# The first queries in two pieces, single-chunk transposes for pair 0, and re-placed row copies in a fused attention and gMLP kernel

## The chip, the cores and the metric

The kernel runs on one core of a Trainium2 chip. A core has TensorE (PE in the profile; PEld is its weight load), VectorE (DVE), ScalarE (ACT), GpSimd (POOL) and SyncE (SP, which here only issues transfers), and 16 DMA engines. The metric is the device time of one execution in microseconds (us); less is better.

## The reference

Block-sparse attention over 4 batches of 8 heads, 768 positions, head size 64, then a gated MLP over the merged heads. The mask works on blocks of 32 positions: 24 by 24 blocks.

```python
scores = scale * np.matmul(q, k.transpose(0, 1, 3, 2))
mask = np.abs(blk_i - blk_j) <= window          # window = 1
mask = mask | (blk_i == 0) | (blk_j == 0) | (blk_i == n_blocks - 1) | (blk_j == n_blocks - 1)
for qb in range(n_blocks):
    for kb in sampled_blocks[qb]:                # 3 sampled blocks for each
        mask[qb * block:(qb + 1) * block, kb * block:(kb + 1) * block] = True
scores = np.where(mask, scores, -1000000000.0)
attn = softmax(scores)
x = (attn @ v), heads merged                     # 4 x 768 x 512
h = np.maximum(x @ w_in, 0.0)                    # u, v = its halves of 512
v_n = (v - mu) / np.sqrt(var + 1e-06)
v_s = np.einsum('ts,bsd->btd', w_spatial, v_n) + b_spatial[None, :, None]
out = (u * v_s) @ w_out
```

## The kernel before

**Layout.** Keys and queries of one head lie in a tile `kq` [128 partitions, 8 heads, 2 x 768 columns]: 64 partitions hold the transposed head vectors (keys in the first 768 columns, queries in the rest), and the other 64 (`MX`) hold mask rows, so that one product of 128 partitions gives score plus mask. The mask rows on the key side are the same for all heads (`K_` columns, a one-hot of the block), and those on the query side are made by products of `bm` with the one-hot rows (`mask_rows`, L268, one for each third of 256 query columns), written into head 0 and copied to the other heads by `rows` (L236). While `mask_rows` uses head 1's columns as its operand, head 1's vector partitions are zero (memset, L173).

**Chunks and pairs.** A head's 768 positions are 6 chunks of 128. Heads are worked in pairs; pair 0 is heads 0 and 1 of batch 0. A load brings float32 rows to `st_k`, `st_q`, `st_v`; a cast makes bfloat16 in `nat`; PE transposes by a product with the identity into PSUM; a DVE copy brings that to `kq`. For pair 0 one transpose takes two chunks of 64 columns at once (`head`, L274), so that even and odd chunks come out in two halves of the partitions and need two copies (`split0`, L280). The load and cast order chunks so that the first four become two runs. Later pairs transpose both heads of a chunk together (`tr_first`, `tr_rest`).

**Order.** The order on each engine is that of the text; a wait stands on the instruction that needs it. The work is cut in slots (the loop at L846). In slots 0 to 35 batch 0 is done in units of three slots: a slot begins with a score product (`qk_unit`, L387), whose four 256-column products of PE are followed by one exp on ACT (L420, 1024 columns; in slot 0 two of 512, L410). Two PSUM buffers hold the scores, so the product of slot s waits for the exp of slot s - 2. Value products (`av_unit`, L444; 24 products of 65 columns in three groups `e` of 8, L458) of the unit follow some slots later; `av_at` (L840) says where: for unit 0 groups 0, 1 and 2 in slots 5, 6 and 6. The functions put in by `when` follow behind them in the slot: `second` (L331: the last two key chunks of head 0) in slot 0, `third` (L337: head 1's keys and first four query chunks) in slot 1, the third mask product in slot 2, `tr_first` of pairs 1, 2, 3 in slots 4, 7 and 9, `tr_rest` of pair 0 in slot 18 (L356, last query third of heads 0 and 1), and the `rows` of later heads (`ROWS`, L733). Units 0 and 1 are heads 0 and 1 with two query thirds; units 2, 3 and 4 are pairs 1 to 3, from slots 6, 9 and 12. From slot 36 on whole heads are worked (L428, L431, L476), and the MLP is dealt in between.

**Queues.** ACT issues the first key load and the first query load (L140, L141); SP issues all else in the order of the text, from L142 on. POOL makes iotas, memsets and the casts, in order (`ORDER`, L304). `filler` products of zeros keep PE busy: 26 ahead, and two at each of three places (`FILL2`). `mhalf` (L172) is the exponent of the MLP's normalization on POOL. The last column of each of six `vv` tiles (values) is set to one (L171), so that the value product also sums the weights.

Of the kernel before, what the change touches and what calls it, by code (L numbers as in the profile page):

```python
# [17 lines left out]
def _listify(ap: bass.AP) -> bass.AP:  # L18
    t = ap.tensor
    if isinstance(t.shape, tuple):  # L20
        t = dataclasses.replace(t, shape=list(t.shape))
        ap = dataclasses.replace(ap, tensor=t)
    return ap
# [3 lines left out]
def kernel(  # L27
# [38 lines left out]
    MOE0 = 12  # L66
    FILL, FILL2 = 26, (2, 2, 2)
    U_DVE = (0, 1, 2, 3, 4, 5)
# [49 lines left out]
    def cast(p, nm, eng, hs=BOTH, cs=ALLC):  # L118
        if nm == "v":
            dst = vv[p % NVV][:, hs, cs, 0:D]  # L120
        else:
            if p not in nat:
                nat[p] = work.tile([128, 2 * NCH, 2, D], BF16, tag="nat", bufs=4, name="nat")
            c0 = 0 if nm == "k" else NCH
            dst = nat[p][:, c0 + cs.start:c0 + cs.stop].rearrange("p c h d -> p h c d")[:, hs]
        src = st[nm, p].rearrange("p h (c d) -> p h c d", d=D)[:, hs, cs]
        if p == 0 and nm != "v":
            dst = nat0_view()[:, hs, (c0 + cs.start) * D:(c0 + cs.stop) * D]
            if cs is not C45:
                dst = dst[:, 0].rearrange("p (i t d) -> p t i d", t=2, d=D)  # L130
                src = src[:, 0].rearrange("p (t i) d -> p t i d", t=2)
            else:
                dst = dst.rearrange("p h (c d) -> p h c d", d=D)
        if eng is nc.scalar:
            nc.scalar.activation(out=dst, in_=src, func=AF.Copy)
        else:
            eng.tensor_copy(out=dst, in_=src)  # L137

    samp = const.tile([KR, 2 * NR], I32)
    load(0, "k", H0, C03, eng=nc.scalar)  # L140
    load(0, "q", H0, C03, eng=nc.scalar)  # L141
    nc.sync.dma_start(out=samp[MR], in_=_listify(sampled_blocks).bitcast(I32))  # L142
    load(0, "k", H0, C45)
    load(0, "k", H1)
# [24 lines left out]
    make_identity(nc, ident)  # L169
    for s in range(NVV):  # L170
        nc.gpsimd.memset(vv[s][:, :, :, D:VA], 1.0)  # L171
    nc.gpsimd.memset(mhalf, -0.5)  # L172
    nc.gpsimd.memset(kq[0:D, 1, 0:TW], 0.0)  # L173

# [69 lines left out]
    act_copy(kq[MX, 0, K_], kq[MX, 1, K_])  # L244
    cast(0, "q", PL, H0, C03)
    cast(0, "k", PL, H0, C45)
# [33 lines left out]
    def split0(ps, h, c0, n, t, copy=dve_copy):  # L280
        w = n * 64
        copy(kq[0:D, h, c0 * 128 + t * w:c0 * 128 + (t + 1) * w], ps[t * D:(t + 1) * D, 0:w])

    K4, K2, Q4 = (0, 2 * TC), (2 * TC, NCH - 2 * TC), (NCH, 2 * TC)
    ps0 = bank()
    head(ps0, 0, *K4)
    split0(ps0, 0, *K4, 0)
    rows(slice(3, 4), K_)
    filler(FILL2[0], wps)
    mask_rows(psum.tile([128, 1024], FP32, tag="sc", bufs=2, name="mq"), 0, act_copy, 1)  # L290
    rows(slice(2, 3), slice(0, 512), nc.scalar)
    filler(FILL2[1], wps)
    psq = bank("psq", "av")
    head(psq, 0, *Q4)
    split0(psq, 0, *Q4, 0)
    split0(ps0, 0, *K4, 1)
    filler(FILL2[2], wps)
    mask_rows(psum.tile([128, 512], FP32, tag=moe_tag(), bufs=1, name="mq"), 1, act_copy, rs=MR)
    split0(psq, 0, *Q4, 1)
    rows(slice(4, 6), K_)  # L300
    rows(H1, qcols(0, 2), PL)
    rows(slice(2, 3), slice(512, S), PL)

# [27 lines left out]
    def second():  # L331
        ps2 = bank("ps2", "av")
        head(ps2, 0, *K2)
        for t in range(2):
            split0(ps2, 0, *K2, t)

    def third():  # L337
        ps1 = bank("ps1")
        head(ps1, 1, 0, NCH)
        head(ps1, 1, *Q4, NCH * 64)  # L340
        for c0, n, at in ((0, NCH, 0), (*Q4, NCH * 64)):
            for t in range(2):
                split0(ps1[:, at:at + n * 64], 1, c0, n, t)

# [8 lines left out]
    def tr_rest(p, t0=1):  # L353
# [3 lines left out]
        if p == 0:  # L357
            for h in range(2):
                head(ps, h, 2 * NCH - 2, 2, h * 128)
            for odd in range(2):  # L360
                dve_copy(kq[0:D, 0:2, S + (NCH - 2 + odd) * 128:S + (NCH - 1 + odd) * 128],
                         ps[odd * D:(odd + 1) * D, 0:256].rearrange("d (h n) -> d h n", h=2))
            return
# [365 lines left out]
    def c(f, *a, **kw):  # L729
        return lambda: f(*a, **kw)  # L730

    K_Q0 = slice(0, S + TW)
    ROWS = [(3, 2, 8, qcols(0)), (5, 6, 8, K_),  # L733
            (15, 4, 6, qcols(1, 2))]
    when(0, second)
    when(4, lambda: rows(slice(6, 8), qcols(1, 2), PL), lambda: casts(-3, None))
# [104 lines left out]
    for u in range(len(UNITS)):  # L841
        for e in range(3):
            sl = (5, 6, 6)[e] if u == 0 else 3 * u + e + (4 if u < 3 else 3)
            av_at.setdefault(sl, []).append((u, e))
    NS = S0 + 12 * (NP - NG)
    for s in range(NS + LAG + 2):  # L846
# [6 lines left out]
        for f in pre.get(s, []):  # L853
            f()
        for u, e in av_at.get(s, []):
            av_unit(u, e)
        if 0 <= s - LAG - S0 and s - LAG < NS:
# [5 lines left out]
        for f in late.get(s, []):  # L863
            f()
        while post:
            post.pop(0)()
# [31 lines left out]
```

## Time and profile before

| | us |
|---|---|
| three runs, median (lowest, highest) | 209.96 (209.9, 210.68) |
| the profiled execution | 210.04 |
| its span, first to last instruction | 208.3 |
| PE busy | 201.0 |
| ACT busy | 168.4 |
| DVE busy | 146.8 |
| POOL busy | 89.4 |

The span is what the profile can show; 1.7 us of the execution lie around it. The granted clock reads 1.00. A busy share is a mean over the whole kernel; at the start, in the first 11 us, no engine is busy throughout, and the parts wait for each other in turn. A row of the timeline shows start, duration, engine, line, operation, output and inputs, shapes, and how many instructions were merged into it; in brackets stands an idle time of the engine ahead of it and what ended it. The rows of the first 11 us, PE's and ACT's in the first 20 us, and DMA's landings are what the change is to be read against.

### The profile page before, as it was taken

Reading aid. Unit: us, or ns where it says so; the run is one execution under the profiler, and the core shown is the slowest. Engines: PE = TensorE matmul, PEld = TensorE weight load, DVE = VectorE, ACT = ScalarE, POOL = GpSimd, SP = SyncE. Lnnn points to the kernel's source line nnn. Section 1 sums busy time; section 2 is a strip of 40 time slices with the busy share of each in tenths; the row PEclk is TensorE's granted clock in tenths of the full one; section 3 lists DMA queues with packets and bytes.
Section 4 is the critical chain, followed back from the end, with each engine's and each line's share of the span. In section 5 each row is a group of like instructions: output and inputs, shape, how many; then the busy total and the mean of one; then the engine's idle time right before and its main releaser. Section 6 shows DMA issues by size and latency. Waiting matters only on the chain.

```text
span 208.3 us, 5489 instructions
## 1 busy us (share of the span) xinstructions
PE 201.0 (97%) x2203; PEld 138.0 (66%) x2225; DVE 146.8 (70%) x315; ACT 168.4 (81%) x222; POOL 89.4 (43%) x186
## 2 busy tenths in 40 slices
PE   6899999999999999999999999999999999999993
PEld 6599888777766776667556676667665567445551
DVE  6888776989876766575975585456875666576871
ACT  6899999999999999989899878889899884266021
POOL 6888989767927964006757600006210000013000
PEclk9999999999999999999999999999999999999999
DMA  5999899999999999499987920499402010610016
GB/s 143 338 362 357 275 383 270 206 247 389 253 253 308 259 300 208 139 199 386 292 176 206 139 41 0 164 189 335 75 0 41 0 37 4 250 57 0 0 70 232
DMA packets 53053, 39.48 MB, mean 190 GB/s; under 512 B 33956, under 2 KB 47652, under 8 KB 53028
## 3 DMA queue, kind: packets, MB, share of 16 engines
q1 hardware_dynamic: 52596, 38.74, 70.0%
q10 hardware_dynamic: 432, 0.39, 0.6%
q8 instruction: 17, 0.28, 0.5%
q14 instruction: 8, 0.07, 0.1%
HBM read 24.77 MB, written 6.29 MB: 149 GB/s over the span
## 4 chain that ended last, share of the span: by engine, by line
PE 87%; DVE 4%; ACT 4%; DMA 2%; issue 1%; POOL 0%; ACTq 0%
PE ps L428 21%; PE ps_moe L630 17%; PE ps_moe L561 13%; PE ps_av L476 12%; PE ps L415 7%; PE ps_av L458 4%; PE ps_t L561 4%; PE ps_t L630 4%; PE ps_sc L630 2%; ACT a_all L420 2%; DVE stats L594 2%; DVE vn L185 2%; DMA st_q<-in_q_dram 2%; PE ps_sc L561 1%; PE ps L263 1%
## 5 line engine op out<-in xcount | busy, mean ns | idle before, releaser
L431 ACT ACTIVATE a_all<-ps 128x768 bf16<-128x768 f32 x144 | 113.4, 812 | 13.8 <-PE ps L428 6.2
L428 PE MATMUL ps<-kq 128*128 128x512 bf16 (+1 forms) x288 | 70.3, 326 | 0.3
L476 PEld LDWEIGHTS <-a_all 128*128 128x128 bf16 x864 | 46.6, 98 | 19.0
L476 PE MATMUL ps_av<-vv,a_all 128*128 128x65 bf16 x864 | 51.1, 194 | 0.1
L428 PEld LDWEIGHTS <-kq 128*128 128x128 bf16 x288 | 27.9, 97 | 23.6
L137 POOL CAST nat<-st_k 128x256 bf16<-128x256 f32 (+3 forms) x37 | 17.7, 509 | 38.7 <-DMA st_k<-in_k_dram 38.7
L420 ACT ACTIVATE a_all<-ps 128x1024 bf16<-128x1024 f32 x35 | 33.5, 1027 | 0.3
L630 PE MATMUL ps_moe<-w_spt,vn 128*128 128x512 bf16 (+1 forms) x144 | 33.1, 325 | 0.0
L598 POOL TENSOR_SCALAR std<-mv 128x3 f32<-128x3 f32 (+1 forms) x9 | 3.4, 376 | 48.7 <-DVE mv L595 48.5
L661 DVE TENSOR_TENSOR sb<-ps_moe,b_row 128x512 f32<-128x512 f32 x18 | 12.4, 690 | 14.5 <-PE ps_moe L630 14.2
L630 PE MATMUL ps_moe<-xt,w_in_t 128*128 128x256 bf16 (+1 forms) x108 | 21.7, 299 | 0.2
L415 PE MATMUL ps<-kq 128*128 128x256 bf16 x135 | 20.8, 275 | 0.8 <-DVE kq L211 0.6
L561 PE MATMUL ps_moe<-w_in_t,xt 128*128 128x512 bf16 x65 | 20.2, 378 | 0.2
L137 POOL CAST vv<-st_v 128x256 bf16<-128x256 f32 (+2 forms) x37 | 18.5, 533 | 3.9 <-DMA st_v<-in_v_dram 3.8
L137 POOL CAST nat<-st_q 128x256 bf16<-128x256 f32 (+2 forms) x41 | 19.2, 496 | 1.6 <-DMA st_q<-in_q_dram 1.5
L561 PE MATMUL ps_moe<-w_out_t,un 128*128 128x512 bf16 x64 | 19.4, 378 | 0.2
L441 DVE TENSOR_TENSOR xn<-ps_av,rc 128x384 bf16<-128x384 f32 (+1 forms) x36 | 18.5, 513 | 1.4 <-DVE rc L440 0.2
L664 DVE TENSOR_TENSOR un<-sb,un 128x512 bf16<-128x512 f32 x24 | 17.4, 727 | 1.5
L630 PEld LDWEIGHTS <-vn 128*128 128x128 bf16 x192 | 15.5, 97 | 4.4
L594 DVE BATCH_NORM_STATS2 stats<-vn 128x6 f32<-128x512 bf16 x24 | 16.5, 688 | 1.5 <-ACT vn L589 0.9
L211 DVE COPY osb<-ps_moe 128x512 f32<-128x512 f32 x12 | 8.3, 689 | 11.2 <-PE ps_moe L561 9.3
L211 DVE COPY kq<-tt 64x1536 bf16<-64x1536 bf16 x24 | 15.4, 641 | 0.6 <-DMA tt<-nat 0.2
(94 smaller groups left out, 241.6 us busy)
## 6 DMA issues: line engine op xcount, KB each, us to landing
out_dram<-osb SPq DMA_DIRECT2D x23, 256.0 KB, 2.1
st_k<-in_k_dram SPq DMA_DIRECT2D x15, 384.0 KB, 4.6
st_v<-in_v_dram SPq DMA_DIRECT2D x15, 384.0 KB, 6.2
st_q<-in_q_dram SPq DMA_DIRECT2D x12, 384.0 KB, 4.9
ws_f<-in_moe_w_spatial_dram SPq DMA_DIRECT2D x6, 384.0 KB, 5.5
w_f<-in_moe_w_in_dram SPq DMA_DIRECT2D x8, 256.0 KB, 6.3
w_f<-in_moe_w_out_dram SPq DMA_DIRECT2D x4, 256.0 KB, 5.4
st_q<-in_q_dram SPq DMA_DIRECT2D x3, 256.0 KB, 6.9
```

What stands on the lines that cost most here:

```text
L137: eng.tensor_copy(out=dst, in_=src)
L211: nc.vector.tensor_copy(out=o, in_=i)
L415: nc.tensor.matmul(out=ps[:, at:at + n * TW], lhsT=kq[:, h, ci * 128:(ci + 1) * 128], rhs=kq[:, h, qcols(t0, n)], start=True, stop=True)
L420: nc.scalar.activation(out=out, in_=ps, func=AF.Exp, scale=0.125)
L428: nc.tensor.matmul(out=ps[:, n0:n1], lhsT=kq[:, j % H, ci * 128:(ci + 1) * 128], rhs=kq[:, j % H, S + n0:S + n1], start=True, stop=True)
L431: nc.scalar.activation(out=a_ref["h", j][:, ci, :], in_=ps[:, 0:S], func=AF.Exp, scale=0.125)
L441: nc.vector.tensor_tensor(out=out, in0=ps[:, :, 0:D], in1=rc[:, 0:n].to_broadcast([128, n, D]), op=ALU.mult)
L476: nc.tensor.matmul(out=av_ref[j][:, qc, :], lhsT=a_ref["h", j][:, ci, qc * 128:(qc + 1) * 128], rhs=vv[p % NVV][:, h, ci, :], start=(ci == ...
L561: nc.tensor.matmul(out=ref["ps"][:, 0:w], lhsT=lhs(i), rhs=rhs(i), start=(i == 0), stop=(i == n - 1))
L594: nc.vector.bn_stats(out=stats, in_=self.vn[:, tcc, :])
L630: nc.tensor.matmul(out=o.rearrange("p (c t) -> p c t", c=n), lhsT=lhs(i)[:, (d0 + x) * 128:(d0 + x + 1) * 128], rhs=rhs(i), start=(i == 0) ...
L664: nc.vector.tensor_tensor(out=self.in_place(*area), in0=sb, in1=self.in_place(*area), op=ALU.mult)
```

## The change

Head 0's first four query chunks come in two loads of two chunks, the first on ACT's queue, the second on SP's, ahead of the keys that SP loads; each has a cast of its own. The two-run order of chunks is kept for head 0's first four key chunks only. The first two mask products, both with head 1's one-hot rows, stand near each other, and the zeroed columns are doubled for that. On ACT both mask copies follow each other without a row copy between them. One filler place goes. Key rows of heads 2 to 7 are copied head by head at more places, all on DVE. Pair 0's later transposes (`second`, `third`, `tr_rest`) take one chunk each (`ones`), so that one copy (`take`) replaces two. The first value group of unit 0 stands at the end of slot 4. Memsets of `vv` 1 to 5 stand with the v casts, and that of `mhalf` in slot 20.

```diff
-    FILL, FILL2 = 26, (2, 2, 2)
+    FILL, FILL2 = 26, (2, 2)
...
         if nm == "v":
             dst = vv[p % NVV][:, hs, cs, 0:D]
+            if 0 < p < NVV:
+                nc.gpsimd.memset(vv[p][:, hs, cs, D:VA], 1.0)
...
-            if cs is not C45:
+            if hs is H0 and cs is C03:
...
     load(0, "k", H0, C03, eng=nc.scalar)
-    load(0, "q", H0, C03, eng=nc.scalar)
+    load(0, "q", H0, C01, eng=nc.scalar)
     nc.sync.dma_start(out=samp[MR], in_=_listify(sampled_blocks).bitcast(I32))
+    load(0, "q", H0, C23)
     load(0, "k", H0, C45)
...
-    for s in range(NVV):
-        nc.gpsimd.memset(vv[s][:, :, :, D:VA], 1.0)
-    nc.gpsimd.memset(mhalf, -0.5)
-    nc.gpsimd.memset(kq[0:D, 1, 0:TW], 0.0)
+    nc.gpsimd.memset(kq[0:D, 1, 0:2 * TW], 0.0)
+    nc.gpsimd.memset(vv[0][:, :, :, D:VA], 1.0)
...
-    cast(0, "q", PL, H0, C03)
+    cast(0, "q", PL, H0, C01)
+    cast(0, "q", PL, H0, C23)
...
+    def ones(ps, h, c0, n, at=0):
+        for i in range(n):
+            tr(ps[0:D, at:at + n * 128], i, nat0_view()[:, h, (c0 + i) * D:(c0 + i + 1) * D])
+
+    def take(ps, h, c0, n):
+        dve_copy(kq[0:D, h, c0 * 128:(c0 + n) * 128], ps[0:D, 0:n * 128])
...
     ps0 = bank()
+    rows(slice(3, 4), K_)
     head(ps0, 0, *K4)
     split0(ps0, 0, *K4, 0)
-    rows(slice(3, 4), K_)
     filler(FILL2[0], wps)
     mask_rows(psum.tile([128, 1024], FP32, tag="sc", bufs=2, name="mq"), 0, act_copy, 1)
-    rows(slice(2, 3), slice(0, 512), nc.scalar)
+    psq = bank("psq", "av")
+    head(psq, 0, NCH, TC)
+    for t in range(2):
+        split0(psq, 0, NCH, TC, t)
+    mask_rows(psum.tile([128, 512], FP32, tag=moe_tag(), bufs=1, name="mq"), 1, act_copy, 1)
+    split0(ps0, 0, *K4, 1)
     filler(FILL2[1], wps)
-    psq = bank("psq", "av")
-    head(psq, 0, *Q4)
-    split0(psq, 0, *Q4, 0)
-    split0(ps0, 0, *K4, 1)
-    filler(FILL2[2], wps)
-    mask_rows(psum.tile([128, 512], FP32, tag=moe_tag(), bufs=1, name="mq"), 1, act_copy, rs=MR)
-    split0(psq, 0, *Q4, 1)
-    rows(slice(4, 6), K_)
+    psr = bank("psr", "av")
+    head(psr, 0, NCH + TC, TC)
+    for t in range(2):
+        split0(psr, 0, NCH + TC, TC, t)
+    rows(slice(2, 3), K_)
     rows(H1, qcols(0, 2), PL)
-    rows(slice(2, 3), slice(512, S), PL)
...
     def second():
         ps2 = bank("ps2", "av")
-        head(ps2, 0, *K2)
-        for t in range(2):
-            split0(ps2, 0, *K2, t)
+        ones(ps2, 0, *K2)
+        take(ps2, 0, *K2)
     def third():
         ps1 = bank("ps1")
-        head(ps1, 1, 0, NCH)
-        head(ps1, 1, *Q4, NCH * 64)
-        for c0, n, at in ((0, NCH, 0), (*Q4, NCH * 64)):
-            for t in range(2):
-                split0(ps1[:, at:at + n * 64], 1, c0, n, t)
+        ones(ps1, 1, 0, NCH + TC)
+        take(ps1, 1, 0, NCH + TC)
+        psr = bank("psr", "av")
+        ones(psr, 1, NCH + TC, TC)
+        take(psr, 1, NCH + TC, TC)
...
             for h in range(2):
-                head(ps, h, 2 * NCH - 2, 2, h * 128)
-            for odd in range(2):
-                dve_copy(kq[0:D, 0:2, S + (NCH - 2 + odd) * 128:S + (NCH - 1 + odd) * 128],
-                         ps[odd * D:(odd + 1) * D, 0:256].rearrange("d (h n) -> d h n", h=2))
+                ones(ps, h, 2 * NCH - TC, TC, h * TW)
+            dve_copy(kq[0:D, 0:2, qcols(2)], ps[0:D, 0:2 * TW].rearrange("d (h n) -> d h n", h=2))
...
-    ROWS = [(3, 2, 8, qcols(0)), (5, 6, 8, K_),
+    ROWS = [(3, 2, 8, qcols(0)), (3, 5, 6, K_), (7, 6, 8, K_),
             (15, 4, 6, qcols(1, 2))]
-    when(0, second)
+    when(0, second, lambda: rows(slice(4, 5), K_))
+    when(20, lambda: nc.gpsimd.memset(mhalf, -0.5))
...
-            sl = (5, 6, 6)[e] if u == 0 else 3 * u + e + (4 if u < 3 else 3)
+            sl = (4, 5, 6)[e] if u == 0 else 3 * u + e + (4 if u < 3 else 3)
...
-        for u, e in av_at.get(s, []):
-            av_unit(u, e)
+        if s > 4:
+            for u, e in av_at.get(s, []):
+                av_unit(u, e)
...
         for f in late.get(s, []):
             f()
+        if s == 4:
+            av_unit(0, 0)
```

## The prediction

> **What bounds the kernel now.** I read the page first, then the chain of waits over the first 40 us, then the timeline of the first 14 us and, row by row, each engine's part of it.
>
> ```profile
> span 208.3 us, 5489 instructions
> PE 201.0 (97%) x2203; PEld 138.0 (66%) x2225; DVE 146.8 (70%) x315; ACT 168.4 (81%) x222; POOL 89.4 (43%) x186
> ```
>
> PE is busy for 97% of the span. Row by row, no PE idle interval after 11.01 us is longer than 0.06 us. So the end of the kernel moves only if PE gets to the work behind 11 us at another time, or if that work grows or shrinks. The change edits this start, and one transpose group at 23 us. The chain of waits (start, duration, what) tells what sets the start:
>
> ```profile
> 1.14 3.19 DMA st_q<-in_q_dram
> ...
> 4.39 0.57 POOL nat L137
> ...
> 5.01 0.30 PE psq L276 x2
> ...
> 5.34 0.30 DVE kq L211
> ...
> 5.68 0.41 PE ps L407 x2
> ...
> 6.11 1.09 ACT a_all L410 x2
> 7.19 3.77 ACT a_all L420 x4
> 10.96 0.04 issue
> 11.01 0.60 PE ps L415 x4
> ```
>
> The reader sees the query load, its cast, its transposes, its copy out of PSUM and the first score product in one line; then six exps back to back; then PE. The timeline shows what stands beside it (start, duration, engine, line):
>
> ```profile
> 4.34 0.36 DVE L241 COPY kq<-kq 64x768 bf16<-64x768 bf16 x1
> ...
> 5.34 0.28 DVE L211 COPY kq<-psq 64x256 bf16<-64x256 bf16 x1 [0.64 <-PE psq L276]
> ...
> 6.77 1.87 DVE L211 COPY kq<-ps 64x128 bf16<-64x128 bf16 x6
> ...
> 7.08 7.67 ACT L420 ACTIVATE a_all<-ps 128x1024 bf16<-128x1024 f32 x8
> ...
> 8.37 1.30 PE L415 MATMUL ps<-kq 128*128 128x256 bf16 x8 [0.57 <-DVE kq L211]
> ```
>
> ACT runs without idle time from 6.11 to 13.7 us. I number exps and score products by their slot. In the trace exps 1 to 8 start at 7.08, 7.98, 9.02, 9.94, 10.84, 11.75, 12.65 and 13.72; where nothing holds them they are 0.905 apart. Score products 5 to 10 start at 10.09, 11.01, 11.95, 13.09, 13.78 and 14.92. Products 6, 9 and 11 to 14 start 0.05 to 0.07 after the exp two slots earlier ends (11.01 after 10.95, 13.78 after 13.71, 18.49 after 18.41), because there are two score buffers. So up to slot 14 ACT and PE bind by turns, and from slot 15 (19.51) PE alone. PE work that is taken out of slots 6 to 14 is worth only what ACT lets through.
>
> **The change, part by part.** *Two query loads (L140 on).* The 128 KB load was issued on ACT's queue at 1.14 and landed at 4.34. Now 64 KB stay there and 64 KB are issued by SP right behind the block list, where the first key load was issued at 1.23 and landed at 4.14. The POOL cast of 128x256 took 0.56; a cast of 128x128 took 0.29 (4.91). I take the first cast to be over by 4.6 and the second by 4.9. Both are then covered, because DVE is busy as follows.
>
> *Row copy first on DVE.* In the changed program's instruction order the row copy of head 3 (0.36) stands ahead of the first key copy. It waits for ACT's L214, which ends at 4.30, so DVE goes: row copy at 4.34, first key copy (64x256, 0.28) at 4.73, the two query copies (64x128, 0.22 each, from the row at 6.77) at 5.05 and 5.30, end 5.52. DVE mostly leaves 0.03 between such rows, which I used; twice it started the next 0.08 before the last ended (5.87 before 5.94). Score product 0 follows its copy by 0.06: 5.58 instead of 5.68, a gain of 0.10. If DVE overlaps throughout and PE waits for nothing else, it is 0.3.
>
> *Mask products together.* The second mask copy on ACT (0.38) can start once the first has ended at 4.66, and is over by 5.4. The row copy on ACT (0.61) goes. Neither was on the chain: ACT sat idle 0.48 before 5.66. Two fillers fewer are two PE rows of 0.06 in idle time. The larger POOL memset (64x512; 0.34 for half) replaces five memsets of vv and mhalf, and POOL waited 1.02 us behind them. At nothing, while that idle time lasts. The vv memsets (0.42 for six) move in front of later v casts, where POOL waits for DMA (0.29 and 0.26 before two of them); mhalf's goes to slot 20, long before its use at 33.4.
>
> *Single-chunk transposes.* `second` issues 2 instead of 1, `third` 10 instead of 5, at 0.056 each (start to start at 6.72). DVE's copies become 1 of 64x256 and one each of 64x1024 (0.68, from 10.16) and 64x256, for six. Product 1 needs the two later query copies: 5.55 first key half, 5.88 and 6.12, end 6.35; it starts at 6.41 and exp 1 at 7.04 (before 7.08). PE then needs 0.44 for product 1 and 0.56 for ten transposes, so product 2 starts at 7.41 and is ready 0.64 later: exp 2 at 8.05 (before 7.98), 0.07 lost. Product 3 waited 0.57 for DVE. Now DVE has row copy, `second`'s copy, row copy (0.36, 0.28, 0.36) from 6.38 and then 0.68, end 8.15, so product 3 runs at 8.21 and exp 3 follows exp 2 without a hole, at 8.95 (9.02).
>
> *First value group a slot earlier.* Eight products of L458 take 0.25 and now stand in slot 4 behind pair 1's eight transposes (0.45). Product 4 starts when exp 2 has ended, 9.13; then 0.44, 0.45 and 0.25 make product 5 start at 10.27 (10.09), exp 5 at 10.91 (10.84). Slot 6 is relieved of 0.25: product 6 at 10.96, but product 7 must wait for exp 5, 11.99 (11.95), then 0.44, 0.45 and 0.25 again: product 8 at 13.13 (13.09). The 0.25 is spent against ACT.
>
> *Last query third at 23 us.* Four transposes for two: +0.11, on PE alone, in full.
>
> The row copies of heads 4 to 8 only change DVE places; their first readers are in slots 9 and 12.
>
> The sum on these numbers is +0.04 at slot 8 and +0.11 at 23 us, +0.15. With the early end of DVE's range all of slots 0 to 8 come about 0.38 earlier against that working, -0.34 at slot 8, and the sum is -0.23. The middle is -0.04. The profiled execution took 210.04 (span 208.3 and 1.7 around it); the median of the runs is 209.96. I forecast no change: 209.9, own range 209.6 to 210.2. I call a difference within 0.5% (1.05 us) no change, about what a measurement of this kernel can tell.
>
> On one point the Trainium skill speaks against the change. The row: POOL's 128x256 cast at 4.39, beside DVE's row copy, took 0.56, the same form at 5.89 took 0.40, so it was slowed by 0.16 and not stopped. The Trainium skill, SBUF — State Buffer, section "SBUF: two separate sides", says that a fast-mode DVE copy and a GpSimd operation exclude each other for the whole instruction. By that rule a cast that finds the row copy running begins at 4.70, the query copies come about 0.3 later, and the sum is +0.45; the trace agrees with a slowing, not with a full stop.
>
> **The rivals.** *Early start, DVE overlapping and the loads on time:* product 0 at 5.38, the row waits of 0.57 and 0.13 gone, and PE's 0.25 fully worth its price: -0.3 - 0.13 - 0.25 + 0.11 = -0.57, 209.4. For it: ACT is free by 5.4. Against: the ten transposes ahead of product 2, and ACT's 0.905 pitch. To reach over 0.5%, noise of the measurement or a stall that I don't see must help.
>
> *Later loads:* SP issues one load more in front, at about 0.43 each, and the DMA share is 0.72 at 4 to 5 us but 0.94 to 1.1 from 5 us on, so what starts later stays later. Pair 3's last cast ends at 13.96 and its transposes stand on PE at 14.48. If everything lands 0.43 later, that cast ends at 14.39; its need in the forecast is 14.5. With a second issue's delay it is 14.82 and PE stalls 0.3; with the 0.15 that is +0.45, 210.4. Against: the queue waits for the eighth load before it, as it did.
>
> *PE falls back to its slow rate; this is the other side.* The first 25 fillers are 0.107 apart, and from 3.6 us on the same form is 0.056 apart, though the granted clock reads 1.00. The change takes two fillers out of the gaps before product 0. If PE drops to the first rate for as long as it had it (2.6 us) from 7 us on, its 1.9 us of work there (0.71 in 7 to 8 us, 0.61 in 8 to 9, 0.55 of the 0.92 in 9 to 10) takes 3.8, the idle 0.7 beside it absorbs part, and 1.2 remain: with 0.15, 211.3. It decides once the idle share before 7 us is large enough; the gap of 0.65 at 4.36 wasn't. The Trainium skill, TensorE: Matmul & The Clock Gate, "Part 1: The HAM clock gate", says that the clock falls after an idle window of about 3.4 us; by that rule the shorter gaps here can't do it.
>
> *The change does not do what its words say:* copies ahead of any rows is true on ACT, not on DVE. That is in the sum already.
>
> **How the numbers follow.** No change by the forecast 0.52; early start 0.18, of which 0.10 over 0.5%; later loads 0.15, of which 0.05 over 0.5%; slow PE 0.13, all over; 0.02 is left to what I don't see. Faster 0.11, within 0.69, slower 0.20. The range reaches from the early start with 0.2% of noise, 209.1, to just short of the slow PE, 211.2.
>
> **What would show it.** DVE's row copy ahead of the key copy, product 0 near 5.5, exp 1 near 7.0, a gap before exp 2 of about 0.1, no DVE wait before product 3, product 8 within 0.4 of 13.1, and 0.11 more between slots 18 and 19. Wrong would be: PE idle over 0.1 us after 11 us, matmul rows 0.107 apart behind 4 us, or pair 3's cast after 14.5.

## The result and the profile after

| | before | changed |
|---|---|---|
| seven runs of each, median us | 210.35 | 211.31 |
| lowest to highest | 209.9 to 211.17 | 210.7 to 211.41 |
| the profiled execution | 210.04 | 210.85 |
| its span | 208.3 | 209.0 |

The ratio is 1.0041, with a 95% interval of 1.0023 to 1.0058; it is formed over all executions, so it can differ from the quotient of the two medians. The change costs about 0.9 us. That is less than the 0.5% within which the prediction spoke of no change, but the interval leaves no doubt about its sign, and the median lies 0.1 above the forecast range, 209.1 to 211.2. Part of the distance to the forecast of 209.9 is the kernel before itself: its median is 210.35 in these seven runs, and was 209.96 in the three from which the forecast started. The two profiled executions differ by 0.81, the medians by 0.96; what the two profiles show is therefore most of it, not all.

The head of the page of the changed kernel, as it was shown of the one before (span, then busy time, share and instructions by engine):

```profile
span 209.0 us, 5501 instructions
PE 202.4 (97%) x2209; PEld 138.7 (66%) x2231; DVE 146.8 (70%) x315; ACT 168.1 (80%) x221; POOL 89.1 (43%) x186
```

PE is still busy for 97%, with 1.4 us more, and its weight loads have 0.7 more; the sums of DVE, ACT and POOL moved by 0.3 at most. The page doesn't say where the time went. It is found by laying the starts of the 180 groups of score products side by side, changed minus before. In us (a product has the number of its slot; these differences are worked out from PE's rows of both timelines):

| product | 0 | 1 | 2 | 3 | 4 | 5 | 6 | 7 to 11 | 12 to 18 | 19 to the last |
|---|---|---|---|---|---|---|---|---|---|---|
| later by | -0.09 | 0.06 | 0.52 | 0.00 | 0.21 | 0.33 | 0.11 | 0.17 | 0.51 to 0.52 | 0.86 |

So there are three steps: 0.17 at the start, and about 0.34 each at product 12 and at product 19. Nothing is lost or won between product 19 and the last one, which is 0.85 late. The last output lands 0.85 late as well (208.14, before 207.29); the closing instructions behind it take 0.91 instead of 0.99, and so the span is 0.77 longer.

The chain of waits of the changed kernel (start, duration, what) passes through all three places:

```profile
6.41 0.54 PE ps L422 x4
6.96 0.56 PE ps L265 x8
7.52 0.66 PE psr L265 x2
8.21 3.87 ACT a_all L427 x4
...
13.92 0.69 DVE kq L212
14.64 1.18 DVE kq L242
16.07 0.42 DVE xn L448
16.49 0.60 DVE kq L212
17.14 0.61 PE ps L422 x4
...
23.73 0.34 PE ps L265 x4
24.07 0.32 PE ps_moe L568
```

First come the ten single-chunk transposes of `third`, which hold up product 2 and so exp 2 at 8.21. Then DVE, which wasn't on the chain after 11 us before, with a row copy of L242 that takes 1.18 and a copy that product 12 waits for. Last the four transposes of `tr_rest`.

**The second step, row by row.** The timeline of the changed kernel around 15 us (start, duration, engine, line, operation, output and input, count, and in brackets an idle time before it and what ended it):

```profile
14.58 0.83 POOL L139 CAST vv<-st_v 128x768 bf16<-128x768 f32 x1 [0.21 <-DMA st_v<-in_v_dram]
...
14.64 1.18 DVE L242 COPY kq<-kq 64x1536 bf16<-64x1536 bf16 x1
...
15.35 0.95 POOL L139 CAST nat<-st_q 128x512 bf16<-128x512 f32 x1
...
15.85 0.18 DVE L447 RECIPROCAL rc<-ps_av 128x4 f32<-128x4 f32 x1
...
16.41 1.40 DVE L212 COPY kq<-ps 64x1024 bf16<-64x1024 bf16 x2
...
17.14 0.39 PE L422 MATMUL ps<-kq 128*128 128x256 bf16 x2 [0.18 <-DVE kq L212]
```

The same copy in the timeline of the kernel before, in slot 5:

```profile
11.59 0.56 DVE L241 COPY kq<-kq 64x1536 bf16<-64x1536 bf16 x1
11.66 1.19 POOL L137 CAST vv<-st_v 128x768 bf16<-128x768 f32 x1 [0.29 <-DMA st_v<-in_v_dram]
```

The key rows of heads 6 and 7 are one copy of 64x1536, and both times it meets a POOL cast of 128x768. Before, DVE was first by 0.07 and took 0.56, and POOL's cast took 1.19 in place of the 0.83 of the other such casts. In the changed kernel POOL was first by 0.06 and took its 0.83, and the DVE copy lasted until 15.82, which is 0.41 after POOL's end. Whoever comes second is stopped, and takes its rest behind the other's end: 0.41 for DVE here, 0.69 for POOL before (12.15 to 12.84). Both rests are about 0.14 shorter than what the instruction takes alone. The rest doesn't depend on how long DVE had stood beside POOL: the same copy started 0.20 and 0.32 behind a POOL cast in two of the runs below, and again ended 0.41 behind the cast's end. If the two only slowed each other, it would. The Trainium skill, SBUF — State Buffer, section "SBUF: two separate sides", says this: the two engines share a pair of ports, and the one that starts first keeps the pair for its whole instruction. Both rows agree with it. Before, DVE won and only POOL, which had time, paid; in slot 7 DVE pays, and behind the copy on DVE stand unit 1's normalization and the first copy of pair 3's transposes (16.41; before 15.23), for which product 12 waits.

How much DVE pays is not fixed by the edit: it depends on when POOL's cast starts, and that moves from one profile to the next. In three of the runs below the changed kernel's copy stands in slot 7 as well, and it took 1.13, 0.78 and 0.57. The 0.57 is from the run with `tr_rest` as before, where the cast of values came behind the copy:

```profile
14.62 0.57 DVE L242 COPY kq<-kq 64x1536 bf16<-64x1536 bf16 x1
...
15.01 0.87 POOL L139 CAST vv<-st_v 128x768 bf16<-128x768 f32 x1 [0.22 <-DMA st_v<-in_v_dram]
```

So 0.34 is what the profiled execution paid, and other executions of the same kernel may pay less.

**The third step.** TensorE's rows around `tr_rest` in the changed kernel, its weight loads (PEld) among them:

```profile
23.20 0.40 PEld L465 LDWEIGHTS <-a_all 128*128 128x128 bf16 x8
23.31 0.42 PE L465 MATMUL ps_av<-vv,a_all 128*128 128x65 bf16 x8
...
23.66 0.25 PEld L265 LDWEIGHTS <-nat 128*64 128x64 bf16 x4
23.66 0.41 PE L265 MATMUL ps<-ident,nat 128*64 128x128 bf16 x4
...
24.00 0.39 PE L568 MATMUL ps_moe<-w_in_t,xt 128*128 128x512 bf16 x1
...
24.23 0.60 PE L422 MATMUL ps<-kq 128*128 128x256 bf16 x4
```

and before:

```profile
23.02 0.13 PEld L276 LDWEIGHTS <-nat 128*128 128x128 bf16 x2
23.05 0.27 PE L276 MATMUL ps<-ident,nat 128*128 128x128 bf16 x2
...
23.16 0.38 PE L561 MATMUL ps_moe<-w_in_t,xt 128*128 128x512 bf16 x1
...
23.38 0.60 PE L415 MATMUL ps<-kq 128*128 128x256 bf16 x4
```

A two-chunk transpose has weights of 128 columns, like all other products here; a single-chunk one has 64 (the 128\*64 of its row) and fills 64 partitions of its output instead of 128; the two always go together here, and "width" stands for both. From the last transpose's start to the MLP's product PE took 0.056 before and 0.152 now; from the last value product to the first transpose 0.034 before and 0.125 now. In the kernel before, the weight load starts ahead of its product (23.02 and 23.05). At the change of width it starts with it (both 23.66): it wasn't taken ahead, and PE stands still for it. So two more transposes cost their 0.11, the two changes of width 0.09 and 0.10, and 0.03 more lies between the first two transposes (0.080 instead of 0.055). The Trainium skill, TensorE: Matmul & The Clock Gate, section "Step-by-step: what each phase is for", says that PE pulls weight loads ahead of running products. The trace agrees between weights of equal width, and not where the width changes.

**The first step** is read from its rows in the same way. TensorE in the changed kernel, slots 1 to 7:

```profile
6.35 0.61 PE L422 MATMUL ps<-kq 128*128 128x256 bf16 x4
6.89 0.63 PE L265 MATMUL ps<-ident,nat 128*64 128x128 bf16 x8
7.36 0.28 PE L265 MATMUL psr<-ident,nat 128*64 128x128 bf16 x2
7.57 0.39 PE L422 MATMUL ps<-kq 128*128 128x512 bf16 x1
...
9.28 0.60 PE L422 MATMUL ps<-kq 128*128 128x256 bf16 x4 [0.30 <-ACT a_all L427]
...
12.12 0.60 PE L422 MATMUL ps<-kq 128*128 128x256 bf16 x4 [0.15 <-ACT a_all L427]
```

and before, slots 1 and 2:

```profile
6.29 0.60 PE L415 MATMUL ps<-kq 128*128 128x256 bf16 x4
6.72 0.44 PE L276 MATMUL ps<-ident,nat 128*128 128x128 bf16 x5
7.04 0.39 PE L415 MATMUL ps<-kq 128*128 128x512 bf16 x1
```

From product 1 to product 2 it is 1.22 (before 0.76); the forecast had 1.00, with 0.109 for each part of product 1 and 0.056 for each transpose. The 0.22 over it are again the change of width: 0.202 from the last part of product 1 to the first transpose (0.109 before), 0.080 from there to the second (0.056), 0.151 from the last transpose to product 2 (0.097 before, 0.056 in the forecast). The wait of 0.57 before product 3 is gone, but exp 2 starts at 8.21, and ACT and PE bind by turns from there: products 4 and 7 wait for exps, as the brackets say. Against the forecast product 4 is 0.15 late, product 7 0.13 and product 8 0.13, so the excess is handed on and not lost. No run takes the change of width alone out of slots 0 and 1: for this step the cause is read from rows, not shown by an experiment.

### The profile page after: what moved, and what is told of

Same layout as the page of the kernel before. It is cut to its first block, busy times and chain, and to the rows that moved or that the text cites. A ratio compares the mean times of both kernels' runs of the same rounds, so it can differ in the third digit from the quotient of the medians.

```text
span 209.0 us, 5501 instructions
## 1 busy us (share of the span) xinstructions
PE 202.4 (97%) x2209; PEld 138.7 (66%) x2231; DVE 146.8 (70%) x315; ACT 168.1 (80%) x221; POOL 89.1 (43%) x186
## 4 chain that ended last, share of the span: by engine, by line
PE 85%; DVE 6%; ACT 5%; issue 1%; ACTq 0%
PE ps L435 21%; PE ps_moe L637 17%; PE ps_moe L568 13%; PE ps_av L483 12%; PE ps L422 6%; PE ps_t L568 4%; PE ps_t L637 4%; PE ps_av L465 3%; PE ps_sc L637 2%; ACT a_all L427 2%; DVE kq L212 2%; DVE stats L601 2%; DVE vn L186 2%; PE ps L265 1%; PE ps_sc L568 1%
## 5 line engine op out<-in xcount | busy, mean ns | idle before, releaser
L139 POOL CAST nat<-st_k 128x256 bf16<-128x256 f32 (+3 forms) x37 | 18.2, 522 | 40.4 <-DMA st_k<-in_k_dram 40.4
L605 POOL TENSOR_SCALAR std<-mv 128x3 f32<-128x3 f32 (+1 forms) x9 | 2.9, 319 | 47.9 <-DVE mv L602 47.7
L668 DVE TENSOR_TENSOR sb<-ps_moe,b_row 128x512 f32<-128x512 f32 x18 | 12.4, 690 | 14.5 <-PE ps_moe L637 14.3
L139 POOL CAST nat<-st_q 128x256 bf16<-128x256 f32 (+3 forms) x42 | 19.6, 497 | 2.3 <-DMA st_q<-in_q_dram 2.3
L139 POOL CAST vv<-st_v 128x256 bf16<-128x256 f32 (+2 forms) x37 | 17.7, 511 | 3.3 <-PE ps_moe L637 1.2
L186 DVE TENSOR_SCALAR vn<-ps_moe 128x512 bf16<-128x512 f32 x18 | 12.4, 687 | 4.3 <-PE ps_moe L568 3.8
```

The costliest lines, as they stand in the source:

```text
L186: nc.vector.tensor_scalar(out=out, in0=in0, scalar1=s1, scalar2=s2, op0=o0, **kw)
```

## The experiments

Offsets are those of the table above, against the profile of the kernel before. Where one execution is said, its profile counts rather than its time. The profile of the kernel before is one execution too: in the run with heads 6 and 7 in slot 7 alone, whose start is the same, the first query load lands at 3.62 instead of 4.34 and products 0 and 1 come 0.13 earlier. So an offset of 0.1 at the first products is not yet an effect of an edit.

**Row copy back in slot 5** (one execution), in the changed kernel:

```diff
-    ROWS = [(3, 2, 8, qcols(0)), (3, 5, 6, K_), (7, 6, 8, K_),
+    ROWS = [(3, 2, 8, qcols(0)), (3, 5, 6, K_), (5, 6, 8, K_),
```

> The changed kernel with one thing undone: the key row copy of heads 6 and 7 stands in slot 5 again, not in slot 7. Theory (place): in the changed kernel that copy took 1.18 us beside a POOL cast instead of 0.56, stood ahead of unit 1's normalization and pair 3's copies on DVE, and product 12 came 0.34 later than by the slots before (offset to the kernel before +0.17 at product 11, +0.51 at product 12). Undone, product 12 should be at about +0.17 and product 35 at +0.51 (it was +0.85). Rival (late data): pair 3's key and query landed 0.4 later and its cast ended at 14.28 instead of 13.96, which delays product 12 in any case: then the offset at product 12 stays near +0.5.

It took 211.28. The wait on DVE before product 12 is gone: the offset goes from 0.71 at product 11 to 0.81 at product 12, where it had been 0.81 at product 10. But PE's rows were still 0.107 apart until 6.65 in this execution, so the start came to 0.60 at product 1 instead of 0.06, and a cost of 0.48 instead of 0.34 stood at product 19, 0.15 of it a wait ahead of that slot's value products. The place of the second step agrees, its size isn't shown by this run. On the port it adds a case: the copy started at 12.35 behind a POOL cast of 12.03 to 12.85 and ended at 13.27, again 0.41 behind POOL. In slot 5 that made product 9 wait 0.10 more, which is taken up again by product 11.

**`tr_rest` with two-chunk transposes** (one execution), in the changed kernel:

```diff
             for h in range(2):
-                ones(ps, h, 2 * NCH - TC, TC, h * TW)
+                head(ps, h, 2 * NCH - 2, 2, h * 128)
+            for odd in range(2):
...
```

> The changed kernel with the last query third of heads 0 and 1 transposed as before (two transposes of two chunks, 128 columns of weights). In the changed kernel the step from product 18 to 19 grew by 0.34. Theory (switch): PE pays about 0.12 each time it goes from weights of 128 columns to weights of 64 and back, on top of 0.11 for two transposes more; undone, product 19 falls back by 0.34. Rival (count): only the number of transposes counts, and the other 0.23 came from something that stands at this place by chance (a late bank or load); undone, it falls back by 0.11.

It took 211.36. The transposes are as before again (0.03 from the last value product to the first transpose, 0.06 from the last transpose to the MLP's product), and the offset grows at product 19 by 0.16 only, which is a wait before the value products in front of them. The total says nothing on that, because another thing happened, which the row of PE shows:

```profile
17.62 0.40 PE L265 MATMUL ps<-ident,nat 128*128 128x128 bf16 x4 [0.90 <-POOL nat L139]
```

A late query third of pair 1 came late, its cast ended at 17.56, and PE waited 0.90 for it: product 12 is 1.22 late where product 11 is 0.15 late.

**`second` and `third` with two-chunk transposes** (one execution), in the changed kernel:

```diff
-        ones(ps2, 0, *K2)
-        take(ps2, 0, *K2)
+        head(ps2, 0, *K2)
+        for t in range(2):
+            split0(ps2, 0, *K2, t)
...
-        ones(ps1, 1, 0, NCH + TC)
-        take(ps1, 1, 0, NCH + TC)
...
+        head(ps1, 1, 0, NCH)
+        head(ps1, 1, *Q4, NCH * 64)
...
```

> The changed kernel with the transposes of slots 0 and 1 as before (two chunks at once, six copies; head 1's chunks cast in the two-run order again). In the changed kernel exp 2 starts at 8.21, not 7.98, because product 2 starts at 7.57 behind ten single-chunk transposes. Theory: with five fewer transposes in slot 1, one fewer in slot 0 and no switch of weight width, product 2 starts by 7.2 and exp 2 at 7.9, held by ACT; but product 3 waits for DVE's five copies again, and exp 3 comes near 8.9 to 9.0. Product 8 then stands within 0.05 of the kernel before (+0.17 in the changed one). Rival (late data): the lost time is the loads' and the row copies', and product 8 stays at +0.15 or more.

It took 210.99, and the expectation failed. Product 2 is back to 0.01, but product 3 waits 0.96 for DVE and exp 3 starts at 9.41; product 3 and products 5 to 11 are about 0.37 late. Two-chunk transposes need two copies for one on DVE, and with the new row copies in front DVE hasn't time for them. The single-chunk form buys that time with PE's. Behind the start this run repeats the other two steps, which it leaves in: 0.29 at product 12, where the copy of heads 6 and 7 took 1.13, and 0.33 at product 19.

**The start alone** (twelve executions): the changed kernel with the three edits above together, `second`, `third`, `tr_rest` and the place of heads 6 and 7 as before:

> The changed kernel with all three undone: row copy of heads 6 and 7 in slot 5, two-chunk transposes in slots 0, 1 and 18. What is left of the change is the start (split query load, mask products together, row copies on DVE) and the first value group in slot 4. Theory: the three steps add, so of +0.85 nothing is left, and with product 0 at 5.6 instead of 5.68 the kernel is at -0.1 to +0.05 of the one before; ratio 0.999 to 1.001. Rival: the start itself costs (loads of pair 1 on land 0.4 later), +0.2 to +0.4 at product 15.

210.53 against 210.33; the ratio is 1.0028 (1.0013 to 1.0043). The profiled execution, the fastest of its twelve with 210.13, has products 0 and 1 earlier by 0.16, product 3 behind a wait of 0.92 on DVE, and 0.08 from product 7 on (0.15 from product 19 on). So the start's new order by itself brings no gain, and its median is further from the kernel before (0.20) than its profile (0.09). The ratio says more than the medians, because four of its twelve executions took over 211 and none of the seventeen of the kernel before did.

**The split query load alone** (twelve executions), in the kernel before, with one cast as there:

```diff
-    load(0, "q", H0, C03, eng=nc.scalar)
+    load(0, "q", H0, C01, eng=nc.scalar)
     nc.sync.dma_start(out=samp[MR], in_=_listify(sampled_blocks).bitcast(I32))
+    load(0, "q", H0, C23)
```

> The kernel before with the query load alone split as in the change (two chunks on ACT's queue, two on SP's behind the block list; one cast after both). Theory (later loads): one more load ahead of all others on SP moves every later one back: pair 2's key, 10.14 before and 10.5 to 10.9 in the five runs with the split, lands at 10.5 or later, pair 2's value at 14.5 or later (14.16), pair 1's late query thirds at 15.4 or later (14.91). The two-chunk start needs these later than it gets them in some executions, so the time is 0.3 to 0.6 us more: ratio 1.0015 to 1.003. Rival (start order): the loads land 0.4 later but have slack, the cost of the start lies in the order of DVE and PE work in slots 0 to 5; then this kernel is at 0.999 to 1.001.

210.17 against 209.98, ratio 1.0012 (1.0000 to 1.0024). In its profile products 0 to 15 are 0.14 to 0.30 earlier, the largest gain at the start in any run here. It is given back at product 16: PE waits 0.13 for the cast of pair 3's late query third, which ends at 20.21 because on POOL it stands behind that of another late third, landed only at 17.41. The offset goes from -0.24 to 0.07, and behind slot 36 further to 0.39. The first load comes sooner, and all that is queued behind the added one comes later.

**The start with the load in one** (twelve executions), the start alone with a single query load:

```diff
-    load(0, "q", H0, C01, eng=nc.scalar)
+    load(0, "q", H0, C03, eng=nc.scalar)
...
-    load(0, "q", H0, C23)
```

> The kernel with three parts undone (row copy in slot 5, two-chunk transposes in slots 0, 1 and 18), and the query load whole again on ACT's queue as well; its two casts, the mask products together, DVE's row copies and the first value group in slot 4 stay. With the split it was 1.0028 [1.0013, 1.0043]. Theory (later loads): the loads land as before (pair 2's key near 10.1), product 0 stays near 5.6, and the ratio falls to 0.998 to 1.000. Rival (start order): the order costs it by itself; the ratio stays at 1.002 to 1.003.

210.52 against 209.98, ratio 1.0032 (1.0020 to 1.0044). Pair 2's keys land as early as before (10.20), and it is no better; the wait of 0.92 before product 3 stays. So the later landings aren't what makes the new start dear. Here too one late query third comes late (landed 16.58, before 14.91):

```profile
17.30 0.40 PE L264 MATMUL ps<-ident,nat 128*128 128x128 bf16 x4 [0.36 <-POOL nat L139]
```

**Heads 6 and 7 in slot 7, alone** (one execution), in the kernel before:

```diff
-    ROWS = [(3, 2, 8, qcols(0)), (5, 6, 8, K_),
+    ROWS = [(3, 2, 8, qcols(0)), (7, 6, 8, K_),
```

> The kernel before with the key row copy of heads 6 and 7 alone moved from slot 5 to slot 7. Theory (place): the copy runs at about 14.5 beside POOL's cast of pair 2's value, takes 0.8 to 1.2 us instead of 0.56, pushes pair 3's first copy from 15.23 to 15.9 or later, and product 12 waits 0.2 to 0.4 for it. Rival: DVE has enough idle time there (0.21 and 0.23 before its rows at 13.0 and 14.7), and product 12 moves by less than 0.1.

210.37. Up to product 11 nothing is later (-0.13 at products 0 and 1, -0.02 from there), and product 12 is 0.17 late, all of it at that one place; from product 37 on it is 0.34, which this run doesn't explain. The timeline:

```profile
14.25 0.83 POOL L137 CAST vv<-st_v 128x768 bf16<-128x768 f32 x1 [0.28 <-DMA st_v<-in_v_dram]
...
14.45 1.03 DVE L241 COPY kq<-kq 64x1536 bf16<-64x1536 bf16 x1
...
16.08 1.40 DVE L211 COPY kq<-ps 64x1024 bf16<-64x1024 bf16 x2
```

One line of the change, put into an otherwise untouched kernel, makes the same copy last 1.03 instead of 0.56 and pair 3's first copy 0.85 later. Product 12 moved by about 0.2, the low end of what was expected, since POOL had started 0.20 ahead of DVE here, and 0.06 in the changed kernel.

**Four transposes of 128 columns in `tr_rest`** (one execution), in the changed kernel. Each takes the last two chunks at once, so that the weights keep their width:

```diff
-                ones(ps, h, 2 * NCH - TC, TC, h * TW)
+                for i in range(TC):
+                    tr(ps[:, h * TW:(h + 1) * TW], i,
+                       nat0_view()[:, h, (2 * NCH - TC) * D:2 * NCH * D])
```

> The changed kernel with four transposes in slot 18 as it has them, but each of two chunks (128 columns of weights); the wrong half is left unused and the last query chunk of heads 0 and 1 takes the one before it, so that part of the output is not the reference's. Theory (switch): same count, no change of weight width: the step from product 18 to 19 falls from 0.34 to 0.11 above the kernel before. Rival (count): it stays near 0.34.

210.51. TensorE around it:

```profile
23.18 0.42 PE L467 MATMUL ps_av<-vv,a_all 128*128 128x65 bf16 x8
23.43 0.39 PE L265 MATMUL ps<-ident,nat 128*128 128x128 bf16 x4
23.65 0.38 PE L570 MATMUL ps_moe<-w_in_t,xt 128*128 128x512 bf16 x1
23.87 0.60 PE L424 MATMUL ps<-kq 128*128 128x256 bf16 x4
```

From the first transpose to the MLP's product it is 0.22, twice the 0.11 of two transposes, and the steps into and out of them are 0.03 and 0.06 as before the change. In the changed kernel the same stretch is 0.34, with 0.125 in front of it. So the count costs 0.11, and the width the rest. The second step is in this run too, with 0.15: the copy took 0.78 there. Product 19 lost 0.25 here all the same, since the first value product of the slot waited 0.14 for a copy.

**Both costs undone** (twelve executions): the changed kernel with the first two edits of this section together, heads 6 and 7 in slot 5 and `tr_rest` with two-chunk transposes:

> The changed kernel with the two costs undone that the profiles put a size on: key row copy of heads 6 and 7 back in slot 5 (0.34 at product 12), last query third by two transposes of two chunks (0.34 at product 19). The split load, the start's order and the single-chunk transposes of slots 0 and 1 stay. Theory (the three steps add): 0.68 us of the 0.85 go, the step at product 12 is under 0.1 unless a late cast holds it, the one at product 19 is under 0.2, and the ratio falls from 1.0041 to 1.0005 to 1.002. Rival (late loads): most of the 1.0041 is executions in which pair 1's late query thirds land behind the instruction fetch; then the ratio stays at 1.003 or more.

210.72 against 210.23, ratio 1.0026 (1.0007 to 1.0045). The profiled execution took 210.18. Its score products are within 0.02 of the changed kernel's up to number 11, at 0.18, and then stay there: 0.18 at product 12, 0.17 at product 19 and at the last. TensorE of this kernel, at the two places:

```profile
16.59 0.38 PE L265 MATMUL ps<-ident,nat 128*128 128x128 bf16 x4
16.81 0.60 PE L424 MATMUL ps<-kq 128*128 128x256 bf16 x4
...
23.22 0.27 PE L278 MATMUL ps<-ident,nat 128*128 128x128 bf16 x2
23.33 0.38 PE L570 MATMUL ps_moe<-w_in_t,xt 128*128 128x512 bf16 x1
23.55 0.60 PE L424 MATMUL ps<-kq 128*128 128x256 bf16 x4
```

Product 12 has no wait in front of it, and the last query third takes what it took. Two edits take 0.68 out of the lateness of the last product (0.66 of the span) and leave what stands ahead of product 12 as it was: the second and the third step of the profiled execution are shown. The ratio didn't fall to the 1.0005 to 1.002 that this had led to expect, nor did it stay at the rival's 1.003. The median is 0.49 above the kernel before where the profile is 0.14 above it.

**Three tries to make the start pay** (five, six and eleven executions). The first is the start alone with the key rows of heads 2 and 4 put behind slot 3:

```diff
-    rows(slice(2, 3), K_)
...
-    ROWS = [(3, 2, 8, qcols(0)), (3, 5, 6, K_), (5, 6, 8, K_),
+    ROWS = [(3, 2, 8, qcols(0)), (3, 2, 3, K_), (3, 4, 6, K_), (5, 6, 8, K_),
...
-    when(0, second, lambda: rows(slice(4, 5), K_))
+    when(0, second)
```

> The kernel with three parts undone (split load kept), and the key row copies of heads 2 and 4 moved from ahead of product 3 to slot 3, where DVE waits 0.6 us for PE. Theory (DVE ahead of product 3): with them ahead, product 3 waited 0.92 us for DVE and exp 3 started at 9.12 instead of 9.02, though exp 2 was 0.17 ahead; without them DVE has 0.8 us less to do there, the wait falls to 0.3 or less, exp 3 starts at 8.8, and products 6 to 10 stand 0.1 to 0.25 ahead of the kernel before; ratio 1.0 to 1.0015 (1.0028 with them). Rival: later loads bind in any case, the offsets at product 12 and 16 and the ratio stay.

210.85 against 210.03, ratio 1.0034 (1.0022 to 1.0046). Exp 3 comes at 8.85 as hoped, and the wait has only moved:

```profile
8.21 1.29 PE L424 MATMUL ps<-kq 128*128 128x256 bf16 x8 [0.66 <-DVE kq L212]
...
11.59 0.61 PE L424 MATMUL ps<-kq 128*128 128x256 bf16 x4 [0.61 <-DVE kq L212]
```

The other two load pair 0's query chunks for both heads together, the one on top of the first try, the other in the kernel before (whose line for the first load has `C03`); on top of the first try the separate load `load(0, "q", H0, C23)` goes as well:

```diff
-    load(0, "q", H0, C01, eng=nc.scalar)
+    load(0, "q", BOTH, C01, eng=nc.scalar)
...
+    load(0, "q", BOTH, C23)
...
-    load(0, "q", H1, C03)
```

> The same with the query loads cut by chunks and not by heads: ACT's queue brings chunks 0 and 1 of heads 0 and 1 (128 KB), SP's chunks 2 and 3 of both (128 KB), so SP issues no load more than in the kernel before. Theory: pair 2's key lands near 10.2 again, not 10.5 to 11.0; fewer executions stall at product 12 or 16; ratio 0.9975 to 1.0. Rival: what the loads lose is set by the instruction fetch at 14 to 15 us alone, whatever the order; ratio as in the run with the rows behind.

> The kernel before with that order of query loads alone. With the split load alone products 1 to 15 stood 0.24 ahead, but loads landed 0.4 later, product 16 lost 0.31, and the ratio was 1.0012 [1.0, 1.0024]. Theory: with no load more on SP the gain of the start stays: ratio 0.998 to 1.0, products 6 to 20 0.1 to 0.25 ahead. Rival: the split gains nothing that lasts; 1.000 to 1.001.

On top of the first try it took 211.79 against 210.03, ratio 1.0077 (1.0064 to 1.0089): head 1's keys land at 6.74, PE waits 0.61 for their cast and later 1.11 for DVE. In the kernel before it took 210.52, ratio 1.0026 (1.0015 to 1.0036): 0.14 early at products 0 and 1, 0.25 late from product 9 on and 0.44 from product 19. Both are misses; no version here beats the kernel before.

## Why the prediction was wrong, by its own steps

**What held.** DVE's row copy went first; product 0 came at 5.59 (forecast 5.58) and exp 1 at 6.99 (7.04). The wait before product 3 went (0.57 to 0.09). The 0.25 of value products in slot 4 was spent against ACT: product 7 waits for exp 5, at 12.12 (11.99). The reading that the end moves only with PE's passage through the first 11 us, and with what is added to PE later, was right for the first and the third step. The loads from pair 2's keys on came 0.36 to 0.44 later, as the rival had it, and pair 3's last cast ended at 14.28, before the 14.5 at which it would have counted, in the profiled execution. Two of the signs of being wrong came: PE stood idle for 0.18 before product 12, and its rows were 0.107 apart until 4.8. The second did no harm here, since product 0 came as forecast.

**The step that failed** is the sentence that the row copies of heads 4 to 8 "only change DVE places". It priced them by their readers, in slots 9 and 12, and by nothing else. What counted was who stands behind the copy on DVE, and which POOL instruction it meets: in slot 7 it meets a cast that starts just before it, lasts 1.18 instead of 0.56, and pushes pair 3's copies past product 12. That is 0.34, and the run with this edit alone shows 0.17 to 0.19 of it from a smaller shift. The one paragraph of the prediction that weighs a full stop against a slowing decided for the slowing, and it weighed one cast on POOL only. It also misread that row: the cast of 4.39 ended at 4.96, 0.26 behind the end of DVE's row copy at 4.70, and 0.26 is the 0.40 that it takes alone less 0.14. That is the rest of a full stop, the same as in the second step, and not a slowing by 0.16. At this place the changed kernel paid only 0.07, on DVE (its row copy took 0.43 beside the cast of keys). Had the full stop been laid against each moved copy, the one in slot 7 would have been found: in the profile before, POOL casts values from 14.22 to 15.05, and DVE would start the copy at about 14.45.

**The terms that were too small** are the single-chunk transposes. Each was priced at the 0.056 that it takes among its own kind. The last query third was put at 0.11 and cost 0.34; in slot 1 the stretch from product 1 to product 2 was put at 1.00 and took 1.22, and product 1 itself came 0.06 early, so that exp 2 came at 8.21 instead of 8.05 and the start cost 0.17 instead of 0.04 at the later slots. What was missing is the change of weight width on both sides, about 0.1 each; a run shows this for the last query third, and for slot 1 it is read from the rows.

**The sum.** The working gave +0.15, and the forecast took the middle between that and a gain through DVE's overlap, -0.04. The working with what was missed is 0.15 + 0.13 + 0.34 + 0.23 = 0.85, less the 0.08 of the closing instructions: the 0.77 by which the span grew. The overlap didn't come: product 0 was where the working without it had it, so leaning to the middle also cost 0.19. The 0.38 by which the early end was to bring everything forward isn't worked out either: the prediction's own rows give product 0 at 5.38 and not at 5.58, which is 0.20. The account holds for the two profiled executions; the medians are 0.96 apart, and what they hold beyond it is open.

**The rivals.** The slow PE was taken to be a fall back from the fast rate. No product of the changed kernel's profile shows one; in the run with the row copy in slot 5 PE was slow until 6.65, and it cost 0.60 at product 1, which is the rate coming late and not falling.

**What stays open.** The profile of the changed kernel is its second shortest execution of seven; five lie between 211.25 and 211.41, 0.4 to 0.6 above it. The run with both costs undone shows the same kind of gap: by the profiles the cost falls from 0.81 to 0.14, by the medians only from 0.96 to 0.49. So about half of what the medians show has no cause here. In three profiles (211.36, 211.07 and 210.37) a late query third was cast 1.6 to 2.0 us later than before; whether that is what the longer executions of the changed kernel have in common isn't shown, as none of them was profiled.

## What to carry to other kernels

Price a moved copy by what stands behind it on its engine and by what the other engine on the shared port is doing at its new time, not by its first reader alone; and where the two start within 0.1 us of each other, expect the price to differ from one execution to the next. The same pair of instructions cost nothing when DVE started first and 0.34 us when POOL did. Price a transpose of another width with both changes of width, and group such transposes rather than scatter them. Where one engine has little spare time in a stretch (DVE ahead of product 3 here), putting its work in another order moves the wait and doesn't remove it.

## What the runs showed of the hardware that was not expected

- Of a VectorE copy within SBUF and a GpSimd instruction, the second to start is stopped, not slowed: five copies of 64x1536 on DVE, alone 0.56, ended 0.41 behind the end of the POOL instruction that they met (in the changed kernel, in the runs with the row copy in slot 5, with heads 6 and 7 in slot 7 alone, with `second` and `third` as before, and once in the kernel before at 9.83), whether they had started 0.06 or 0.32 behind it. VectorE's copies out of PSUM go on beside GpSimd: the one at 13.21 in the changed kernel took its 0.68 beside a cast of 13.11 to 13.94.
- A change of weight width between 128 and 64 columns stops TensorE for about 0.09 to 0.10 us, each way; in the rows the weight load there starts with its product and isn't taken ahead. Four transposes of full width in the same place show none of it.
- The time at which PE's rows go from 0.107 to 0.056 apart differs by execution, with the same fillers in front: at 3.7 us in the profile before, behind 4.8 in that of the changed kernel, behind 6.6 with the row copy back in slot 5. An order of the start that profits from PE's speed at 5 us is worth different things in different executions.
- In the stretch from 12 to 18 us each of the profiles has one packet of instruction code among the transfers; the table of DMA queues of the changed kernel there (packets, MB, share of the 16 engines):

```profile
q1 hardware_dynamic: 1977, 2.18, 107.4%
q8 instruction: 1, 0.02, 1.2%
```

  1.2% of 16 engines over 6 us is 1.15 us of one engine. It starts at 14.05 in the changed kernel and at 15.01 before. It may have to do with the late query thirds, but the profiles without a late third have it too, and no run took it away.
